# Some squares of batch 0's scores to Pool between its DMA issues, and the last weight blocks ahead of batch 1's second half

## The chip, the cores and the metric

The kernel runs on one core of one Trainium2 chip. The metric is the device time of one execution in microseconds. Before the change five runs took 436.14, 439.96, 436.26, 435.78 and 436.40 us, with a median of 436.26 us. Beside these there is one profiled execution, with its trace.

## The reference

Attention with squared ReLU in place of softmax, and behind it a gated feed-forward layer (FFN):

```
q, k, v: 8 batches x 12 heads x 448 x 64, float32
scores = (1/sqrt(64)) * q @ k^T
attn   = max(scores, 0)**2 / 448
x      = attn @ v                          # heads side by side: 3584 x 768
xn     = x / sqrt(mean(x*x) + 1e-6) * rms_g
h      = silu(xn @ w_gate) * (xn @ w_val)  # 3584 x 1536
out    = h @ w_out                         # 3584 x 768
```

There is no maximum and no sum over a row of scores, so a piece of scores can be rectified and squared alone, and used.

## The kernel before

**Tiling.** Heads go in pairs, six per batch. The two heads of a pair lie on the two halves of the 128 partitions, so that two 64-row matmuls run side by side in the array. Keys of a head are cut in three chunks of 128 and a rest of 64. Batch 0 is worked in two column halves of 224 queries (`NA`); batches 1 to 7 in one piece of 448.

**Stages of a batch.** q and k are transposed: for batches 0 and 1 by TensorE (`psT`), later ones by DMA. A unit of scores (`psS`, L869, two banks of PSUM wide) or the scores with the key rests of two pairs (`psR`, L890) is rectified into an SBUF tile `r` (L810 on VectorE or L812 on ScalarE), and `r` is squared in place (L818, VectorE alone: `SQ_ACT` is empty). A visit (`visit_aux`) takes two head pairs and multiplies their squares with v (`psAV`, L976); so a batch has three visits, and a half of batch 0 has three too. A visit has two halves with a hand-over between them; where the next visit's psR can be computed, it stands between the halves. What comes out is scaled into `xT`, its squares are summed (`psSS`), ScalarE makes `rstd`, and VectorE makes the six `xn` products (L1132). Then the FFN: `psg` and `psv` per block of 128 of the 1536 columns, `silu` on ScalarE (L1194), the product `hT` on VectorE (L1210), and the output projection `psO`.

**What sets the order.** The order of all engines is fixed while the program is built, by the class `Planner`. It holds estimated costs and due times and plays the engines forward: `choose` picks TensorE's next piece (visits first, then units of scores that are due, then the FFN stream), `engine_next` gives each elementwise task to an engine among those in its cost table. Until the first FFN matmul, TensorE is given filler matmuls (`psB`, L1481) where the planner sees a hole of more than `GAP` ns.[...]

**Loads.** All loads that cast from float32 to bfloat16 are issued by Pool, in the order of `FIRST`, then `ORDER`, then the two halves of `w_out`. In `ORDER`, `w0-2` is two 128-column blocks of both `w_gate` and `w_val` (786 KB read for each), `k` and `K` are the first and second half of batch 1's heads of k and q (three transfers each), and `v` is batch 1's v (two transfers). `issue` lets at most eight be in flight: each waits until the one eight places ahead of it has landed. Of batch 1, pairs 0 to 2 come with `k` and pairs 3 to 5 with `K`; all three visits need `v`.

**Banks.** PSUM starts with three wide buffers for scores and visits and two FFN banks. `warm` (L1492) turns the third wide buffer into two more FFN banks when the first half of batch 0 has had `THIRDV` visits.

Of the kernel before, what the change touches and what calls it, by code (L numbers as in the profile page):

```python
# [10 lines left out]
ALU = mybir.AluOpType  # L11
ACT = mybir.ActivationFunctionType
# [15 lines left out]
def latest(toks, at=0.0):  # L28
    for k in toks:
        if k.t is None:  # L30
            return None
        at = max(at, k.t)
    return at
# [21 lines left out]
class Planner:  # L55
# [2 lines left out]

    SEM, PSUM, HAND, SW = 50.0, 210.0, 200.0, 95.0
    WARM = 6500.0  # L60
    GAP = 160.0
    either = ("square", "squared")
    SLACK = 0.0
    PEN = 200.0
    acts = ("relu",)

# [23 lines left out]
    def engine_next(self):  # L90
        best = None
        for item in self.tasks:
            prio, seq, cost, emit, need, out, then = item
            r = latest(need)
            if r is None:
                continue
            for e in cost:
                s = max(r, self.free[e])
                if prio >= 2 and s + cost[e] > self.reserve[e] + 150.0:
                    continue  # L100
                if item[3].__name__ in self.either and e == "act" and s + cost[e] > max(r, self.free["dve"]) + cost["dve"] + self.SLACK:
                    continue
                key = (s + (self.PEN if e == "dve" and "act" in cost and item[3].__name__ in self.acts else 0.0), prio, seq)
                if best is None or key < best[0]:
                    best = (key, item, e, s)
        return best
# [155 lines left out]
    def choose(self, t):  # L262
# [21 lines left out]
        for a in self.auxes + self.sneaks:  # L284
            r = a.ready()
            if r is not None:
                times.append(r)
        if self.warm() and (not times or min(times) > t + self.GAP):
            return t, self.filler
# [51 lines left out]
def kernel(  # L341
# [11 lines left out]
    nc = tc.nc  # L353
# [18 lines left out]
    DUE1 = 1  # L372
    OLDSQ = 1
    SQ_ACT = range(0, 0)
    NA = 224
    HOLD = 900.0
    JOIN = 300.0
# [6 lines left out]
    W0 = (A2, A2, A3)  # L384
    WE = (A2, A2, A3)
    WO = (A2, A2, A2, A2)
    ORDER = "w0-2 w2-4 k w4-6 w6-8 w8-10 K w10-12 v"
    FIRST = "k4-8 q8-12 k8-12 v0-4 v4-12 Q"
    F32_T = 2
    AGATE = 6  # L390
    THIRD = 0
    THIRDV = 3
    CHAINS = range(0, 0)

    ctx.enter_context(tc.manual_schedule())
# [23 lines left out]
    def act_cost(n, per=0.8333):  # L419
        return 172.0 + per * n  # L420

    def dve_cost(n, per=1.0417):
        return 156.0 + per * n
# [98 lines left out]
    def load_k0(h0, h1):  # L522

        t = new_k0()

        def go():
            nc.gpsimd.dma_start(  # L527
                out=t[:, h0:h1], in_=src_of["k"][0, h0:h1].rearrange("h (p u) d -> p h (u d)", p=D)
            )

        landed("k", 0, h0, h1, issue(go, S * (h1 - h0) * D * 4, U * D * 4))
# [5 lines left out]
    def load_v(b, h0, h1, need=()):  # L537
        load_runs("v", b, h0, h1, low, 0, UH, need)
        load_runs("v", b, h0, h1, high, UH - 1, U, need)
# [76 lines left out]
    def free_bank(bank):  # L616
        def then(end):
            bank.free = end + 60.0
        return then
# [173 lines left out]
    live = {"r": 0}  # L793
    WR = max(S, max(n * min(512 // n, UH - 1) for n in (NA, S - NA)))
    xTs, x2s, accs, rstds, xns, hTs = {}, {}, {}, {}, {}, {}
    subs = [Sub(0, 0, NA, 0.0), Sub(0, NA, S - NA, 0.0)]
    subs += [Sub(b, 0, S, 0.0 if b < 2 else PACE) for b in range(1, B)]
# [3 lines left out]
    def rectify(sub, ps, bank, w, ready, put):  # L801

        got = {}
        tok = Tok()

        def relu(e):
            r = apool.tile([P, 2, WR], BF16, name="r", tag="r")
            got["r"] = r
            if e == "dve":
                nc.vector.tensor_relu(out=r[:, :, :w], in_=ps[:, :, :w])  # L810
            else:
                nc.scalar.activation(out=r[:, :, :w], in_=ps[:, :, :w], func=ACT.Relu)  # L812
            put(r, tok)

        def square(e):
            r = got["r"]
            if e == "dve":
                nc.vector.tensor_tensor(out=r[:, :, :w], in0=r[:, :, :w], in1=r[:, :, :w], op=ALU.mult)  # L818
            else:
                nc.scalar.activation(out=r[:, :, :w], in_=r[:, :, :w], func=ACT.Square)  # L820

        a = pl.task(
            PRIO_R, {"act": act_cost(2 * w), "dve": dve_cost(2 * w)}, relu, [Tok(ready)],
            None, free_bank(bank),
        )
        cost = {"dve": dve_cost(2 * w, 0.52)}
        if sub.b in SQ_ACT:
            cost["act"] = act_cost(2 * w, 0.9)
        pl.task(PRIO_R, cost, square, [a], tok)

    class Unit:
# [14 lines left out]
        def begin(self):  # L846
            sub, n = self.sub, self.sub.n
            bank = take_wide()
            ps = bank.take("psS")
            live["r"] += 1  # L850
            ends = []
            total = 2 * len(self.parts)
            w = n * len(self.parts)

            def put(r, tok):
                for j, c, o in self.parts:
                    sub.r[j, c] = (r, o, tok)

            def cb(t):
                ends.append(t)  # L860
                if len(ends) == total:
                    rectify(sub, ps, bank, w, max(ends), put)

            t = qkT[sub.b]
            for hh in range(2):
                prt = (low, high)[hh]
                for j, c, o in self.parts:
                    def emit(hh=hh, prt=prt, j=j, c=c, o=o):
                        nc.tensor.matmul(  # L869
                            out=ps[:, hh, o : o + n], lhsT=t[prt, j, 0, c * P : (c + 1) * P],  # L870
                            rhs=t[prt, j, 1, sub.q0 : sub.q0 + n], start=True, stop=True,
                        )
                    pl.ins[hh].append((n, emit, cb, 0.0))
# [7 lines left out]
    def rest_scores(sub, k, s):  # L881

        bank = take_wide()
        ps = bank.take("psR")
        live["r"] += 1
        n, t = sub.n, qkT[sub.b]
        for hh in range(2):
            prt = (low, high)[hh]
            for jj in range(2):
                nc.tensor.matmul(  # L890
                    out=ps[jj * D : (jj + 1) * D, hh, :n],
                    lhsT=t[prt, 2 * k + jj, 0, (UH - 1) * P : (UH - 1) * P + D],
                    rhs=t[prt, 2 * k + jj, 1, sub.q0 : sub.q0 + n],
                    start=True, stop=True,
                )

        def put(r, tok):
            sub.rest[k] = (r, tok)

        rectify(sub, ps, bank, n, s + n / 2.4 + pl.PSUM, put)  # L900
        sub.ready_rest[k] = True
# [462 lines left out]
    for x in FIRST.split():  # L1364
# [4 lines left out]
        else:  # L1369
            h0, h1 = [int(y) for y in x[1:].split("-")]  # L1370
            load_k0(h0, h1) if x[0] == "k" else load_v(0, h0, h1)
    for x in ORDER.split():
        if x[0] == "w":
# [118 lines left out]
    def warm():  # L1492
        if third in wide and getattr(subs[THIRD], "visited", 0) >= THIRDV and third.free is not None:
            wide.remove(third)
            early.close()
            psum_y = ctx.enter_context(
                tc.tile_pool(name="psum_y", bufs=1, space=bass.MemoryType.PSUM)
            )
            for x in range(2, 4):
                banks.append(Bank(psum_y, "m%d" % x, [P, 512]))  # L1500
                banks[-1].free = max(third.free, max(pl.t))
        return 0 not in started
# [33 lines left out]
```

## Time and profile before

| | |
|---|---|
| median of five runs | 436.26 us |
| profiled execution | 437.3 us, of it the profiled span 435.5 us |
| TensorE busy | 429.7 us (99%) |
| VectorE busy | 264.9 us (61%) |
| ScalarE busy | 251.8 us (58%) |
| Pool busy | 78.2 us (18%) |
| first FFN matmul | 24.66 us into the span |
| first visit of batch 1 | 52.46 us, held until 53.69 us |
| first FFN matmul of batch 1 | 84.18 us |

In the rows of the profile, an operation is named by line, engine, output <- inputs, then partitions x elements and type; "busy, mean ns of one" follow, and behind the last bar the idle time of the engine just before such operations and what ended it. In the chain and the timeline the first number is the start in us from the span's beginning and the second the length. TensorE's two half-array streams overlap, so matmuls in the timeline are longer than the slot by which they advance. A DMA row in the chain runs from issue to landing. In the rows with one digit per slice, the span is cut in 40 slices of 10.9 us, and a digit is the busy share in tenths.

### The profile page before, as it was taken

What the parts mean: (1) busy time and instruction counts of PE and PEld (TensorE: products, weight loads), DVE (VectorE), ACT (ScalarE), POOL (GpSimd) and SP (SyncE); (2) the same over time, 40 slices, a digit from 0 to 9 for tenths busy, and PEclk for the clock granted to TensorE, in tenths of its full rate; (3) what the DMA queues carried; (4) which work ended last, traced back from release to release, by engine and by line L of the source; (5) the groups of instructions that cost most, each with busy time, mean ns of one, the idle gap of its engine ahead of it and who ended that gap; (6) DMA issues with size and microseconds to landing.
All of it is one profiled execution on the core that took longest, in us unless ns stands there. A gap on an engine that the chain in (4) does not pass through costs nothing.

```text
span 435.5 us, 12544 instructions
## 1 busy us (share of the span) xinstructions
PE 429.7 (99%) x5573; PEld 314.8 (72%) x5573; DVE 264.9 (61%) x437; ACT 251.8 (58%) x356; POOL 78.2 (18%) x97
## 2 busy tenths in 40 slices
PE   8999999999999999999999999999999999999996
PEld 6688678964579755885579855795569955699996
DVE  3898873468754676657844578567754577442200
ACT  4878873576653675657743677476744567442222
POOL 7544311062160070005200340001000000000000
PEclk9999999999999999999999999999999999999999
DMA  9999999699799599188917992157103200020023
GB/s 146 192 197 197 203 193 115 133 166 124 114 152 203 118 137 66 38 133 105 129 38 158 143 158 16 32 124 94 28 14 100 74 2 2 2 74 2 2 74 108
DMA packets 134805, 44.68 MB, mean 103 GB/s; under 512 B 104096, under 2 KB 131296, under 8 KB 134752
## 3 DMA queue, kind: packets, MB, share of 16 engines
q0 software_dynamic: 94448, 24.16, 57.3%
q1 hardware_dynamic: 39808, 19.50, 21.7%
q8 instruction: 43, 0.70, 0.6%
q10 hardware_dynamic: 496, 0.24, 0.2%
q14 instruction: 10, 0.08, 0.1%
HBM read 48.76 MB, written 11.01 MB: 137 GB/s over the span
## 4 chain that ended last, share of the span: by engine, by line
PE 87%; DMA 11%; POOL 1%; issue 1%; ACT 0%; POOLq 0%
PE psO L147 26%; PE psv L147 24%; PE psg L147 23%; PE psAV L976 8%; PE psS L869 5%; DMA vb<-in_v_dram 3%; DMA wg_sb<-in_moe_w_gate_dram 3%; DMA wv_sb<-in_moe_w_val_dram 3%; DMA k<-in_k_dram 2%; PE psR L890 1%; PE psSS L1082 0%; POOL wg_sb L575 0%; POOL qb L496 0%; POOL k L527 0%; ACT ost L1288 0%
## 5 line engine op out<-in xcount | busy, mean ns | idle before, releaser
L147 PE MATMUL psv<-xn,wv_sb 64*128 64x448 bf16 (+1 forms) x1296 | 170.8, 329 | 0.0
L147 PE MATMUL psg<-xn,wg_sb 64*128 64x448 bf16 (+1 forms) x1296 | 170.2, 329 | 0.0
L812 ACT ACTIVATE r<-psS 128x896 bf16<-128x896 f32 x133 | 118.9, 919 | 32.8 <-PE psS L869 32.0
L147 PE MATMUL psO<-wo_sb,hT 64*128 64x384 bf16 (+2 forms) x1464 | 132.3, 310 | 0.0
L147 PEld LDWEIGHTS <-hT 64*128 64x128 bf16 x1464 | 109.9, 94 | 14.6 <-issue 2.5
L147 PEld LDWEIGHTS <-wv_sb 64*128 64x128 bf16 x1296 | 93.7, 94 | 31.8 <-issue 2.8
L147 PEld LDWEIGHTS <-wg_sb 64*128 64x128 bf16 x1296 | 94.8, 94 | 30.2 <-issue 2.9
L818 DVE TENSOR_TENSOR r<-r 128x896 bf16<-128x896 bf16 (+1 forms) x171 | 99.8, 610 | 11.1 <-ACT r L812 10.6
L1210 DVE TENSOR_TENSOR hT<-sil,psv 128x448 bf16<-128x448 bf16 x96 | 59.3, 618 | 62.5 <-PE psv L147 62.2
L1194 ACT ACTIVATE sil<-psg 128x448 bf16<-128x448 f32 x96 | 52.3, 545 | 47.8 <-PE psg L147 47.5
L869 PE MATMUL psS<-qkT 64*128 64x448 bf16 (+1 forms) x324 | 53.0, 329 | 0.0
L1288 ACT COPY ost<-psO 128x384 f32<-128x384 f32 (+2 forms) x51 | 23.0, 451 | 50.2 <-PE psO L147 50.0
L508 POOL DMA_DIRECT2D vb<-in_v_dram x18 | 13.1, 742 | 180.6 <-PE psg L147 75.3
L976 PE MATMUL psAV<-r,vb 64*64 64x448 bf16 (+1 forms) x756 | 43.5, 336 | 1.2 <-DMA vb<-in_v_dram 0.8
L1007 DVE TENSOR_SCALAR xT<-psAV 128x896 bf16<-128x896 f32 (+1 forms) x20 | 20.4, 1022 | 25.9 <-PE psAV L976 25.8
L812 ACT ACTIVATE r<-psR 128x896 bf16<-128x896 f32 (+1 forms) x23 | 19.6, 852 | 28.7 <-PE psR L890 28.7
L1132 DVE SCALAR_TENSOR_TENSOR xn<-xT,g_sb,rstd 128x448 bf16<-128x448 bf16 (+1 forms) x54 | 30.2, 628 | 7.8 <-ACT rstd L1116 7.7
L976 PEld LDWEIGHTS <-vb 64*64 64x64 bf16 x756 | 18.5, 106 | 21.6 <-PE psAV L976 8.5
L555 POOL DMA_DIRECT2D kb<-in_k_dram x42 | 31.5, 798 | 13.9 <-DMA vb<-in_v_dram 6.3
L869 PEld LDWEIGHTS <-qkT 64*128 64x128 bf16 x324 | 19.1, 94 | 9.7 <-issue 0.9
L810 DVE TENSOR_SCALAR r<-psS 128x896 bf16<-128x896 f32 x11 | 12.0, 1089 | 17.5 <-PE psS L869 17.4
L1032 DVE TENSOR_TENSOR x2f<-xT 128x896 f32<-128x896 bf16 x18 | 19.5, 1085 | 2.0 <-ACT xT L1005 2.0
(55 smaller groups left out, 176.3 us busy)
## 6 DMA issues: line engine op xcount, KB each, us to landing
vb<-in_v_dram POOLq DMA_DIRECT2D x14, 384.0 KB, 6.4
kb<-in_k_dram POOLq DMA_DIRECT2D x42, 96.0 KB, 7.3
qb<-in_q_dram POOLq DMA_DIRECT2D x6, 672.0 KB, 10.1
out_dram<-ost SPq DMA_DIRECT2D x7, 336.0 KB, 2.8
wg_sb<-in_moe_w_gate_dram POOLq DMA_DIRECT2D x6, 384.0 KB, 13.2
wv_sb<-in_moe_w_val_dram POOLq DMA_DIRECT2D x6, 384.0 KB, 13.2
wo_sb<-in_moe_w_out_dram POOLq DMA_DIRECT2D x2, 1152.0 KB, 19.3
out_dram<-ost SPq DMA_DIRECT2D x8, 288.0 KB, 2.9
```

The source lines that it names most:

```text
L147: mm = self.nc.tensor.matmul(out=seg.bank["tile"][:, off : off + seg.w], lhsT=lhsT[prt], rhs=rhs[prt], start=(seg.first and h == 0 and i = ...
L555: lambda o=o, i=i: nc.gpsimd.dma_start(out=o, in_=i),
L812: nc.scalar.activation(out=r[:, :, :w], in_=ps[:, :, :w], func=ACT.Relu)
L818: nc.vector.tensor_tensor(out=r[:, :, :w], in0=r[:, :, :w], in1=r[:, :, :w], op=ALU.mult)
L869: nc.tensor.matmul(out=ps[:, hh, o : o + n], lhsT=t[prt, j, 0, c * P : (c + 1) * P], rhs=t[prt, j, 1, sub.q0 : sub.q0 + n], start=True, st ...
L976: mm = nc.tensor.matmul(out=ps[hh * D : (hh + 1) * D, jj, :n], lhsT=vt[prt, 2 * (ja + jj) + hh, u * D : (u + 1) * D], rhs=r[prt, hh, o : o ...
L1007: nc.vector.tensor_scalar_mul(out=xT[at], in0=ps[:, :, :n], scalar1=inv_attn)
L1032: nc.vector.tensor_tensor(out=got["x2"][:], in0=xT[at], in1=xT[at], op=ALU.mult)
L1132: nc.vector.scalar_tensor_tensor(out=xn[:, kt, q0 : q0 + n], in0=xTs[b, 0][:, kt, q0 : q0 + n], scalar=g_sb[:, kt : kt + 1], in1=rstd[:, q ...
L1194: nc.scalar.activation(out=s[:, :m], in_=ps[:, :m], func=ACT.Silu)
L1210: nc.vector.tensor_tensor(out=h[:, fbs[0] : fbs[-1] + 1, o : o + n], in0=s[:, :m].rearrange("p (f s) -> p f s", s=n), in1=ps[:, :m].rearra ...
L1288: nc.scalar.copy(out=ost[:, c0 : c0 + w], in_=ps[:, :w])
```

## The change

A square of a batch in `SQ_POOL` (batch 0) may now be done by Pool too, at an estimated 105 + 1.755 ns an element in the planner's table. Pool takes one only where the planner sees it done no later than 400 ns (`POOL_SLACK`) after VectorE could have had it. In `ORDER`, `w10-12` changes places with `K`. Fillers are put in only for holes of more than 210 ns instead of 160, and the third wide buffer is given up after two visits instead of three.

```diff
-    GAP = 160.0
+    GAP = 210.0
     SLACK = 0.0
+    POOL_SLACK = 400.0
...
+                if e == "pool" and "dve" in cost and s + cost[e] > max(r, self.free["dve"]) + cost["dve"] + self.POOL_SLACK:
+                    continue
...
+    SQ_POOL = range(0, 1)
...
-    ORDER = "w0-2 w2-4 k w4-6 w6-8 w8-10 K w10-12 v"
+    ORDER = "w0-2 w2-4 k w4-6 w6-8 w8-10 w10-12 K v"
...
-    THIRDV = 3
+    THIRDV = 2
...
         def square(e):
             r = got["r"]
-            if e == "dve":
-                nc.vector.tensor_tensor(out=r[:, :, :w], in0=r[:, :, :w], in1=r[:, :, :w], op=ALU.mult)
+            if e == "act":
+                nc.scalar.activation(out=r[:, :, :w], in_=r[:, :, :w], func=ACT.Square)
             else:
-                nc.scalar.activation(out=r[:, :, :w], in_=r[:, :, :w], func=ACT.Square)
+                (nc.vector if e == "dve" else nc.gpsimd).tensor_tensor(
+                    out=r[:, :, :w], in0=r[:, :, :w], in1=r[:, :, :w], op=ALU.mult
+                )
...
+        if sub.b in SQ_POOL:
+            cost["pool"] = 105.0 + 1.755 * 2 * w
```

In the order that the planner now makes, Pool has four squares: the first (128x448) behind the second k transfer of `k`, the second (128x896) between the gate and the value weights of `w6-8`, the third (128x448) between those of `w10-12`, the fourth (128x448) between the two k transfers of `K`. Each is read by another visit of batch 0. TensorE has six filler matmuls fewer. From 41 us on, the transposes of batch 1's pairs 3 and 4 stand together and later, those of pair 5 stand behind batch 1's first visit, and FFN matmuls stand where they and some scores were. From batch 1's third visit on, TensorE's order is the old one. On VectorE and ScalarE the order changes with it, and some transposes' copies, rectifications and squares of `xT` change engine.

## The prediction

> **What bounds the kernel now.** The page comes first: what sets the end, and what else is full.
>
> ```profile
> PE 429.7 (99%) x5573; PEld 314.8 (72%) x5573; DVE 264.9 (61%) x437; ACT 251.8 (58%) x356; POOL 78.2 (18%) x97
> ...
> PE   8999999999999999999999999999999999999996
> ...
> DMA  9999999699799599188917992157103200020023
> ```
>
> TensorE has work in every slice; its idle time is 435.5 - 429.7 = 5.8 us, so a change that leaves TensorE's work alone can win only idle time, filler matmuls and changes between array shapes. But the DMA row is also full for the first six slices (10.9 us each). So I read the chain of work that ended last, in order of time, for the first 55 us:
>
> ```profile
> 4.11 6.66 DMA k<-in_k_dram
> ...
> 11.86 13.16 DMA wv_sb<-in_moe_w_val_dram
> ...
> 25.31 13.20 DMA wg_sb<-in_moe_w_gate_dram
> ...
> 38.79 14.85 DMA vb<-in_v_dram
> 53.64 0.04 issue
> 53.69 0.99 PE psAV L976 x14
> ```
>
> Until 53.64 us the chain is transfers, one behind the other: each is issued when the one eight places ahead of it has landed, and it lands 13 to 15 us later because the queue in front of it is that long. The last link is batch 1's v, whose second half lands at 38.79 + 14.85 = 53.64 us. From there on the chain is TensorE without a hole. The timeline of TensorE shows the meeting point:
>
> ```profile
> 52.46 0.38 PE L976 MATMUL psAV<-r,vb 64*64 64x448 bf16 x2
> 53.69 1.79 PE L976 MATMUL psAV<-r,vb 64*64 64x448 bf16 x26 [0.84 <-DMA vb<-in_v_dram]
> 55.28 0.39 PE L890 MATMUL psR<-qkT 64*64 64x448 bf16 x4
> 55.60 0.56 PE L147 MATMUL psv<-xn,wv_sb 64*128 64x224 bf16 x8
> ```
>
> Batch 1's first visit of the values (I call it AV1) comes up at 52.46 us, issues two matmuls and then stands until 53.69. **The end is therefore 53.69 us plus TensorE's work behind that point**, 435.53 - 53.69 = 381.8 us. What makes TensorE earlier at AV1 is worth nothing; what moves work from behind AV1 to ahead of it is worth its slots. Last, the windows by stage (columns: length, then busy time of PE, PEld, DVE, ACT, POOL):
>
> ```profile
> 0.00:24.66 24.66, 23.22 (x366) 15.85 (x367) 16.33 (x35) 16.94 (x24) 15.60 (x26) 1.00 1.30 172
> 24.66:40.00 15.34, 15.34 (x323) 12.49 (x324) 13.42 (x26) 10.95 (x16) 6.89 (x9) 1.00 1.46 197
> 40.00:53.64 13.64, 12.84 (x242) 10.35 (x238) 13.30 (x25) 12.54 (x18) 5.39 (x7) 1.00 1.40 200
> 53.64:86.61 32.97, 32.80 (x547) 27.72 (x549) 17.60 (x29) 17.86 (x25) 3.76 (x3) 1.00 1.27 148
> ```
>
> VectorE is 87% busy from 24.66 to 40 us and 98% until v lands, then 53%. A VectorE delay before 53.64 can reach TensorE; behind it there is room.
>
> **The change, part by part.** From the two built orders, engine by engine:
>
> (a) *Fillers.* Six of 75 filler matmuls go (9 to 5, 4 to 3, 17 to 16 in three runs between 15.67 and 24.66 us). Seventeen of them fill 22.88 to 24.66 us, 0.105 us each, so 0.63 us less TensorE time. All of it lies ahead of AV1, so alone it is worth 0: the wait for v grows by as much.
>
> (b) *Work on either side of AV1.* Behind AV1 the new order has 28 fewer 64x224 FFN matmuls, 4 more 64x448 score matmuls and 16 more transposes (head pair 5 of batch 1). Slots: two 224-wide matmuls advance by 0.096 us in the timeline, two 448-wide by 0.19; a block of 16 transposes takes from 44.42 to 44.97 us and, with the change of array shape in front, 0.62. So 28 x 0.048 = 1.34 us leave, 4 x 0.095 = 0.38 and 0.62 come: **-0.34 us behind AV1**. Ahead of it the same amounts come with the other sign, less about 0.19 because two pairs are now transposed in one block (one return to the other shape saved): +0.15 us.
>
> (c) *AV1 itself.* Now its two halves stand together and the four psR matmuls come after them; 53.69 to 55.60 is 1.91 us, its two first matmuls (0.09) having been done before. In the new order psR stands between the halves, as at 59.38 to 61.12 us: 1.74 us for all. Gain 1.91 - (1.74 - 0.09) = **0.26 us**, behind the landing.
>
> (d) *Last weights ahead of batch 1's second half of k and q.* Bytes ahead of v are the same, so v should land where it does, at 53.6 us. The weights for the last FFN blocks landed at 35.38 + 13.54 = 48.9 us and now land about 3.1 us earlier, which no one needs. The second half of k and q landed at 30.80 + 13.43 = 44.23 us; the pair of weights takes 48.92 - 44.23 = 4.7 us in the queue, so it lands at about 48.9 us. It is needed by the double block of transposes. TensorE reaches AV1 at 52.46 - 0.63 + 0.15 = 52.0 us if nothing holds it; between that block and AV1 stand 48 FFN matmuls (2.30 us), 4 score matmuls (0.38) and the block (1.0): it comes up at 48.3 us and waits about 0.6 to 0.7 us. TensorE then reaches AV1 at 52.7, still 0.9 us ahead of v. Cost 0 while that cover stands; without it 0.7 us. Queued behind the block on VectorE is one copy of it and, behind this, an hT product that frees an FFN bank: the same 0.7 us, same cover. Head pair 5 is transposed behind AV1, and its scores are needed by the third visit some 13 us later: 0.
>
> (e) *Four squares to Pool*, three of 128x448 and one of 128x896. The rows:
>
> ```profile
> L818 DVE TENSOR_TENSOR r<-r 128x896 bf16<-128x896 bf16 x165 | 97.6, 619 | 10.8 <-ACT r L812 10.3
> ...
> L818 DVE TENSOR_TENSOR r<-r 128x448 bf16<-128x448 bf16 x6 | 2.3, 386 | 0.4 <-ACT r L812 0.3
> ```
>
> VectorE loses 3 x 0.386 + 0.619 = 1.78 us of work. No such square runs on Pool. Below, Pool could be as fast as VectorE (0.39, 0.62). The nearest row is Pool's one elementwise operation on 128x128 in 0.29 us, 2.3 ns an element: 1.0 us for 448 and 2.0 us for 896, an estimate, which I take. Pool's queue holds them: the timeline of Pool (start, length, what, idle before) around the first two:
>
> ```profile
> 13.60 0.67 POOL L508 DMA_DIRECT2D kb<-in_k_dram  x1 [0.25 <-DMA vb<-in_v_dram]
> 15.36 0.77 POOL L496 DMA_DIRECT2D qb<-in_q_dram  x1 [1.09 <-DMA vb<-in_v_dram]
> ...
> 21.26 0.82 POOL L575 DMA_DIRECT2D wg_sb<-in_moe_w_gate_dram  x1 [1.13 <-DMA wv_sb<-in_moe_w_val_dram]
> 23.32 0.82 POOL L575 DMA_DIRECT2D wv_sb<-in_moe_w_val_dram  x1 [1.24 <-DMA wg_sb<-in_moe_w_gate_dram]
> ```
>
> The first square fits 14.27 to 15.36, the second runs 22.5 to 24.5 and makes the issue at 23.32 about 1.2 us late, the last two (rectified about 27.5 and 32 us) fall behind issues of 27 and 31 us. Those transfers land 13 us after issue because others are in front: an issue 1 to 2 us late only finds a shorter queue. Cost of the moved issues 0; that cover is 13 us thick. Their readers are four batch-0 visits; the first, now at 16.66 us and 0.4 us earlier without the four fillers, has its square at 15.3.
>
> [...] By VectorE's rows alone the step frees 1.78 us of VectorE. [...] 3 x 1.0 + 2.0 - 1.78 = +3.2 us of VectorE delay, the worst at 22.9 us, where six xn products gate the first FFN matmul at 24.66. TensorE has 53.6 - 52.0 = 1.6 us to lose before v lands[...]. I take 0: partial collisions, under the cover.
>
> (f) The earlier turn of one score bank into two FFN banks, and the new planner constants: nothing beyond the orders above. Sum: -0.34 - 0.26 = **-0.6 us**. The profiled span goes from 435.5 to 434.9, the profiled execution from 437.3 to 436.7; the median of the runs shown from 436.26 to 435.7.
>
> **Rivals.**
>
> *R1[...].* Pool's squares hold up VectorE, and through xn and the batch-0 squares TensorE. It decides from 1.6 us of TensorE lateness on. At the full 3.2 us: 435.7 + 1.6 = 437.3 us, slower than before; beyond 0.5% (2.2 us) only from 4.4 us, that is with Pool squares well over 2 us each. For it: VectorE 87 to 98% busy there.[...]
>
> *R2, k and q too late.* If their second half lands 2 us or more behind my 48.9, or the copies behind it stack up, AV1 comes after v: each us over the 0.9 of cover costs one. About 437.0. For it: landings here vary by 0.8 us for equal sizes (13.2 to 14.8). Against: the cover.
>
> *R3, v is not a wall.* If the new queue order lands v up to 1.6 us earlier, fillers and wait are won as well: 435.7 - 1.6 = 434.1. Against: same bytes, full queue.
>
> *R4, the change does nothing that counts*: VectorE's relief is hidden, the order shifts cancel, 436.3.
>
> **How the numbers follow.** The likeliest case 0.60 (435.7, give or take 0.7), R1 0.17, R2 0.09, R3 0.06, R4 0.08. About 0.5% (2.2 us) is what a measurement can tell from no change: faster is below 434.1, half of R3 and some of the likeliest case's edge, 0.06; slower is above 438.4, the ends of R1 and R2 (half of their 0.26), 0.13; same 0.81. The range holds the likeliest case, R4 and most of R1 and R2: 434.8 to 437.8.
>
> **What would show it.** Right: AV1 still waits for v at about 53.6 us; a short TensorE wait near 48.3 us for batch 1's q; behind AV1 about 381.2 us; Pool squares near 1 and 2 us. Wrong: v landing elsewhere, AV1 without a wait for v, VectorE squares and xn products stretched or idle beside Pool's squares by more than 1.6 us in all, or TensorE holes behind 54 us.

## The result and the profile after

The changed kernel takes 438.07 us, a median over 44 runs (the runs of the kernel before on the same chips: 436.29 us). The ratio is 1.0046, with a 95% interval of 1.0029 to 1.0063: about 1.8 us slower, where 0.6 us faster was forecast. Some executions of every version, the kernel before included, took 3 to 8 us longer at a mean granted clock of 0.98 to 0.99, and ratio and interval rest on most of these too, so a ratio here need not be that of the two medians. Its profiled execution took 437.63 us, its span 435.8 us.

The page of the changed kernel shows how busy each engine was, and TensorE's row of 10.9 us slices:

```profile
PE 429.1 (98%) x5567; PEld 314.5 (72%) x5567; DVE 268.1 (62%) x434; ACT 250.9 (58%) x355; POOL 83.3 (19%) x101
...
PE   8999999999999999999999999999999999999996
```

VectorE has three operations fewer than before (434 for 437), four squares of 1.78 us in all left it, and yet it is busy *longer*: 268.1 us for 264.9. By itself this says little, because other work changed engine too: VectorE has two more squares of `xT` in float32 (`x2f`, 20 for 18, 21.7 us for 19.5). The clearer sign is the chain of work that ended last, in order of time. Before, it ran through transfers until v landed at 53.64 us. Now:

```profile
14.16 1.04 DVE x L1026
15.20 1.01 DVE r L814
16.25 0.35 PE psB L1489 x2
...
23.07 3.61 DVE xn L1140 x6
26.72 0.83 PE psg L150 x7
```

Two stretches of VectorE have entered it, at 12 to 16 us and at 22.5 to 26.7 us, and no transfer stands in it behind these. The timeline of TensorE at batch 1's first visit (AV1 in the prediction):

```profile
54.49 0.95 PE L984 MATMUL psAV<-r,vb 64*64 64x448 bf16 x16
55.27 0.36 PE L898 MATMUL psR<-qkT 64*64 64x448 bf16 x4
55.50 0.79 PE L984 MATMUL psAV<-r,vb 64*64 64x448 bf16 x12
```

It begins at 54.49 us and shows no wait. v was issued at 38.54 and landed 13.3 us later, at 51.8 us, so 2.7 us ahead of its reader. The two halves of the visit stand around psR as forecast. From AV1's third matmul to the end of the span TensorE needs 381.35 us; before it was 381.85 us. So the work behind AV1 is 0.50 us shorter, close to the 0.60 us that the prediction counted, and all of the loss lies ahead of AV1. None of the waits that end TensorE's idle times in this trace ends with Pool: TensorE does not wait for the squares themselves.

Pool's timeline, with its four squares (in brackets the idle time before, and what ended it):

```profile
13.71 1.23 POOL L824 TENSOR_TENSOR r<-r 128x448 bf16<-128x448 bf16 x1 [0.19 <-DVE r L814]
...
22.63 1.98 POOL L824 TENSOR_TENSOR r<-r 128x896 bf16<-128x896 bf16 x1 [0.78 <-DVE r L814]
...
29.22 0.93 POOL L824 TENSOR_TENSOR r<-r 128x448 bf16<-128x448 bf16 x1 [1.32 <-ACT r L816]
...
33.64 0.93 POOL L824 TENSOR_TENSOR r<-r 128x448 bf16<-128x448 bf16 x1 [1.99 <-ACT r L816]
```

The estimates of 1.0 and 2.0 us were right. Beside these, VectorE's timeline:

```profile
13.54 0.61 DVE L824 TENSOR_TENSOR r<-r 128x896 bf16<-128x896 bf16 x1
14.07 1.12 DVE L1026 TENSOR_TENSOR x<-xT 128x448 bf16<-128x448 bf16 x1
...
22.99 3.68 DVE L1140 SCALAR_TENSOR_TENSOR xn<-xT,g_sb,rstd 128x224 bf16<-128x224 bf16 x6
26.59 1.68 DVE L824 TENSOR_TENSOR r<-r 128x896 bf16<-128x896 bf16 x3
...
29.67 0.72 DVE L1026 TENSOR_TENSOR x<-xT 128x448 bf16<-128x448 bf16 x1
```

In the kernel before, the same operations (lines L1018, L1132 and L818 there) read:

```profile
14.41 0.39 DVE L1018 TENSOR_TENSOR x<-xT 128x448 bf16<-128x448 bf16 x1
...
22.91 2.26 DVE L1132 SCALAR_TENSOR_TENSOR xn<-xT,g_sb,rstd 128x224 bf16<-128x224 bf16 x6
25.09 2.22 DVE L818 TENSOR_TENSOR r<-r 128x896 bf16<-128x896 bf16 x4
```

In this trace one operation of VectorE beside each of Pool's squares is held until about 0.25 us after that square: the square of `xT` at 14.07 us took 1.12 instead of 0.39 us, the six xn products 3.68 instead of 2.26 us (the first of them 1.87 instead of 0.44), the square of `xT` at 29.67 us 0.72, and one at 34.15 us 0.67 instead of 0.39. Together VectorE was held 0.73 + 1.42 + 0.34 + 0.28 = 2.77 us, against 1.78 us of work taken off it. What VectorE had begun 0.15 to 0.21 us ahead of a square of Pool's kept its length: two squares their 0.61 us, at 13.54 and 22.46 us, and two copies out of PSUM (`xT<-psAV`), at 29.01 and 33.49 us, their 0.63 and 0.62. It seems to go the other way too: Pool's first square began while VectorE's square of 13.54 us was running, and took 1.23 us where the later ones of its size took 0.93.

### The profile page after: what moved, and what is told of

Read it like the earlier page. It is cut to its first block, busy times and chain, and to the rows that moved or that the text cites. A ratio compares the mean times of both kernels' runs of the same rounds, so it can differ in the third digit from the quotient of the medians.

```text
span 435.8 us, 12535 instructions
## 1 busy us (share of the span) xinstructions
PE 429.1 (98%) x5567; PEld 314.5 (72%) x5567; DVE 268.1 (62%) x434; ACT 250.9 (58%) x355; POOL 83.3 (19%) x101
## 4 chain that ended last, share of the span: by engine, by line
PE 95%; DVE 2%; DMA 1%; issue 0%; ACT 0%; POOLq 0%
PE psO L150 26%; PE psv L150 26%; PE psg L150 25%; PE psAV L984 9%; PE psS L877 6%; PE psT L676 1%; DMA k<-in_k_dram 1%; PE psR L898 1%; DVE xn L1140 1%; DVE r L814 0%; DVE r L824 0%; DVE x L1026 0%; PE psSS L1090 0%; PE psT L674 0%; PE psB L1489 0%
## 5 line engine op out<-in xcount | busy, mean ns | idle before, releaser
L824 DVE TENSOR_TENSOR r<-r 128x896 bf16<-128x896 bf16 (+1 forms) x167 | 98.1, 614 | 11.1 <-ACT r L816 10.6
L816 ACT ACTIVATE r<-psR 128x896 bf16<-128x896 f32 (+1 forms) x24 | 20.5, 855 | 32.6 <-PE psR L898 31.7
L1015 DVE TENSOR_SCALAR xT<-psAV 128x896 bf16<-128x896 f32 (+1 forms) x21 | 21.5, 1025 | 28.2 <-PE psAV L984 28.2
L1140 DVE SCALAR_TENSOR_TENSOR xn<-xT,g_sb,rstd 128x448 bf16<-128x448 bf16 (+1 forms) x54 | 31.7, 654 | 7.8 <-ACT rstd L1124 7.7
L1040 DVE TENSOR_TENSOR x2f<-xT 128x896 f32<-128x896 bf16 x20 | 21.7, 1085 | 2.0 <-ACT xT L1013 2.0
## 6 DMA issues: line engine op xcount, KB each, us to landing
wv_sb<-in_moe_w_val_dram POOLq DMA_DIRECT2D x6, 384.0 KB, 13.5
```

The costliest lines, as they stand in the source:

```text
L824: (nc.vector if e == "dve" else nc.gpsimd).tensor_tensor(out=r[:, :, :w], in0=r[:, :, :w], in1=r[:, :, :w], op=ALU.mult)
L1015: nc.vector.tensor_scalar_mul(out=xT[at], in0=ps[:, :, :n], scalar1=inv_attn)
L1040: nc.vector.tensor_tensor(out=got["x2"][:], in0=xT[at], in1=xT[at], op=ALU.mult)
L1140: nc.vector.scalar_tensor_tensor(out=xn[:, kt, q0 : q0 + n], in0=xTs[b, 0][:, kt, q0 : q0 + n], scalar=g_sb[:, kt : kt + 1], in1=rstd[:, q ...
```

## The experiments

Each ran beside the kernel before, whose median in these comparisons is 436.19 to 436.28 us. The theory: Pool's squares hold VectorE, through it TensorE, and in an ordinary execution there is no wait for v to hide that. From the load order alone to the kernel with no square for Pool, each expectation gives this theory's figure first. Against it stand that the new orders of loads and matmuls delay TensorE (order theory), that visits wait for Pool's slower squares (late-result theory), that the squares hurt by making Pool's DMA issues late, and that v still sets the end and lands later. Some versions do work, beside that of the reference, that nobody reads.

**The kernel before, profiled a second time** (no edit).

> The kernel before, unchanged, for another profile of it. Question: is batch 1's v a wall in an ordinary execution? The profiled execution of before took 437.3 us, 1.0 us over the median of all its runs (436.3), and TensorE stood 1.2 us for v. Theory A (v is no wall as a rule): a profile near 436.2 us shows no wait for v, or one under 0.3 us. Theory B (v is a wall): the wait of about 1 us is there at any time. Ratio 1.000 for both.

436.22 us, ratio 0.9996 [0.9965, 1.0028], profiled execution 435.96 us with a span of 434.2 us. TensorE's timeline of it at AV1 (28 matmuls in one piece, and no wait in brackets):

```profile
51.60 0.78 PE L147 MATMUL psv<-xn,wv_sb 64*128 64x224 bf16 x12
52.30 1.81 PE L976 MATMUL psAV<-r,vb 64*64 64x448 bf16 x28
```

v was issued at 39.01 us and landed 13.3 us later, at 52.3 us, just as TensorE came up. The 1.2 us stand at AV1 in the profile shown with the prediction belonged to that one execution, whose 437.3 us were 1.0 us above the kernel's median. The work behind AV1 is 381.85 us in both.

**The load order alone.**

```diff
-    ORDER = "w0-2 w2-4 k w4-6 w6-8 w8-10 K w10-12 v"
+    ORDER = "w0-2 w2-4 k w4-6 w6-8 w8-10 w10-12 K v"
```

> The kernel before with the new load order alone (last weights ahead of batch 1's second half of k and q); no squares on Pool, old filler gap, old bank turn. [...] (the whole loss comes from Pool's squares holding up VectorE): 0 to -0.5 us, 435.8 to 436.3. Order theory (late k and q hold up the transposes and what follows): +1 us or more, 437.3 to 438.

436.20 us, 0.999 [0.9959, 1.0021], span 434.1 us. The second half of q landed at 48.0 us and TensorE did not stand for it. The load order is not the cause.

**All but the load order and the two planner constants.**

```diff
-    GAP = 210.0
+    GAP = 160.0
...
-    ORDER = "w0-2 w2-4 k w4-6 w6-8 w8-10 w10-12 K v"
+    ORDER = "w0-2 w2-4 k w4-6 w6-8 w8-10 K w10-12 v"
...
-    THIRDV = 2
+    THIRDV = 3
```

> The changed kernel with the old load order, the old filler gap and the old bank turn: squares on Pool alone. The planner puts the fourth square behind the first k transfer of the second half. [...] 437.5 to 438.3 us, with the xn products of batch 0's first half at 3.5 us for six in place of 2.3. Order theory: no change, 436.3.

437.84 us, 1.0048 [1.0021, 1.0075], span 436.4 us: 1.6 of the 1.8 us in the medians, and within its interval all of them, from the squares on Pool and the TensorE order that follows from them. The six xn took 3.7 us here too.

**The changed kernel, its squares put back on VectorE where they stand.** The planner still plans them for Pool, so TensorE's order is that of the changed kernel.

```diff
-                (nc.vector if e == "dve" else nc.gpsimd).tensor_tensor(
+                nc.vector.tensor_tensor(
```

> The changed kernel, TensorE's order and Pool's DMA order unchanged, but the four squares planned for Pool are issued on VectorE at the same places. [...] Pool holds nothing, VectorE gets 1.8 us of work back; 435.6 to 436.4 us. Order theory: as the changed kernel, 438.0. Late-result theory (readers wait for the slow Pool squares, VectorE isn't touched): 435.6 to 436.4 as well[...].

436.58 us, 1.0021 [0.9987, 1.0056], span 434.3 us. With the same TensorE order, 1.5 us of the 1.8 us are gone when Pool doesn't do the squares. How TensorE loses them can be followed up to the first FFN block. Executions begin unequally: the twelve `psS` near 13.5 us begin ahead of every square on Pool and of every filler that went, and already stand 0.35 us apart in the rows below, so times are counted from there. TensorE's timeline in the kernel before (second profile):

```profile
13.69 0.88 PE L869 MATMUL psS<-qkT 64*128 64x224 bf16 x12
...
24.49 0.27 PE L147 MATMUL psg<-xn,wg_sb 64*128 64x224 bf16 x1
...
24.81 1.21 PE L147 MATMUL psg<-xn,wg_sb 64*128 64x224 bf16 x11
25.86 0.35 PE L147 MATMUL psv<-xn,wv_sb 64*128 64x224 bf16 x2
```

In this one, with the new order and the squares on VectorE:

```profile
13.34 0.88 PE L877 MATMUL psS<-qkT 64*128 64x224 bf16 x12
...
23.96 0.27 PE L150 MATMUL psg<-xn,wg_sb 64*128 64x224 bf16 x1
...
24.43 1.61 PE L150 MATMUL psg<-xn,wg_sb 64*128 64x224 bf16 x11
25.88 0.35 PE L150 MATMUL psv<-xn,wv_sb 64*128 64x224 bf16 x2
```

And in the changed kernel, where the bracket gives the idle time before the first and what ended it:

```profile
13.53 0.88 PE L877 MATMUL psS<-qkT 64*128 64x224 bf16 x12
...
25.00 0.25 PE L150 MATMUL psg<-xn,wg_sb 64*128 64x224 bf16 x1 [0.35 <-DVE xn L1140]
...
25.29 2.26 PE L150 MATMUL psg<-xn,wg_sb 64*128 64x224 bf16 x11
27.39 0.35 PE L150 MATMUL psv<-xn,wv_sb 64*128 64x224 bf16 x2
```

The block's gate matmuls need the xn products one after the other. In the kernel before the first one starts 10.80 us behind the twelve psS and the psv matmuls 12.17 us behind them. With the squares on VectorE the first one starts after 10.62 us, 0.18 us earlier, by the fillers that went. But psv comes after 12.54 us, 0.37 us later, for the large square, at the place where it was planned for Pool, now stands between the first xn product and the other five. VectorE's timeline of that kernel:

```profile
22.37 0.45 DVE L1140 SCALAR_TENSOR_TENSOR xn<-xT,g_sb,rstd 128x224 bf16<-128x224 bf16 x1
22.73 0.62 DVE L824 TENSOR_TENSOR r<-r 128x896 bf16<-128x896 bf16 x1
23.26 1.90 DVE L1140 SCALAR_TENSOR_TENSOR xn<-xT,g_sb,rstd 128x224 bf16<-128x224 bf16 x5
```

With the squares on Pool the first gate matmul starts after 11.47 us, the eleven behind it take 2.26 us, and psv comes after 13.86 us: 1.32 us later than with the squares on VectorE, 1.69 us later than in the kernel before. In the medians the two kernels with the same TensorE order are 1.49 us apart (438.07 against 436.58 us).

**Only the three squares of 128x448 on Pool.**

```diff
-        if sub.b in SQ_POOL:
+        if sub.b in SQ_POOL and w == NA:
```

> The changed kernel, but only the three 128x448 squares may go to Pool; the 128x896 square stays on VectorE. TensorE's order as in the changed kernel. [...] the 896 square is the one that meets the xn products (about 1.6 us of TensorE holes at 25 to 26.7 us of some 2.6), so 436.2 to 436.9 us. If the other squares cost as much: 437.5 or more.

436.67 us, 1.002 [0.9991, 1.005], span 435.0 us. In the medians it is not to be told from the one with all squares on VectorE (+0.1 us). Its six xn took 2.25 us. In its profile the small squares do hold VectorE, though: beside the first one, five squares took 3.67 us instead of 2.52:

```profile
15.21 3.67 DVE L824 TENSOR_TENSOR r<-r 128x896 bf16<-128x896 bf16 x5
```

Its psv came 12.99 us behind the twelve psS, 0.45 us later than with all squares on VectorE.

**Only the square of 128x896 on Pool**, the others issued on VectorE.

```diff
-                (nc.vector if e == "dve" else nc.gpsimd).tensor_tensor(
...
+                (nc.gpsimd if e == "pool" and w != NA else nc.vector).tensor_tensor(
```

> TensorE's order and the plan of the changed kernel; only the 128x896 square runs on Pool, the three of 128x448 are issued on VectorE at the same places. [...] the changed kernel (438.1) less the three small squares, which cost about 0.1 to 0.3 us (all on VectorE: 436.6; small ones alone on Pool: 436.7): 437.6 to 438.1, with the xn products at 3.6 us for six. If the large square isn't the one: 436.6 to 437.0.

437.69 us, 1.0024 [0.9993, 1.0054], span 435.8 us. Pool's timeline of it, and then VectorE's:

```profile
22.52 1.82 POOL L827 TENSOR_TENSOR r<-r 128x896 bf16<-128x896 bf16 x1
```

The six products beside it:

```profile
22.72 3.68 DVE L1143 SCALAR_TENSOR_TENSOR xn<-xT,g_sb,rstd 128x224 bf16<-128x224 bf16 x6
```

The one square stretches the six xn by as much as all four did. Its psv came 13.42 us behind the twelve psS: 0.9 of the 1.32 us by which the squares on Pool delay it come from this square, and the other 0.4 us, at the first visit behind it, from the first small one. By the medians it carries 1.1 of the 1.5 us; the intervals overlap, so the rows carry this reading more than the medians do.

**The kernel before, with four products added on Pool that nobody needs.** They stand at the places of the four squares, read and write a tile of their own, and wait for nothing but Pool's queue.

```diff
+    scr = const.tile([P, 2 * S], BF16, name="scr", tag="scr")
+    nc.vector.memset(scr[:], 1.0)
+    def beside(n):
+        nc.gpsimd.tensor_tensor(out=scr[:, :n], in0=scr[:, :n], in1=scr[:, :n], op=ALU.mult)
...
+            if nm == "k" and b == 1 and (h0 == 0) == (u0 == UH):
+                beside(S)
...
+                if dst is wg_sb and f0 in (6, 10):
+                    beside(2 * S if f0 == 6 else S)
```

> The kernel before with four Pool products on a scratch tile that nobody reads (448, 896, 448 and 448 elements), put between the DMA issues near where the changed kernel has its squares; VectorE keeps all its squares. [...] VectorE's two-input operations are stretched beside them; 437.0 to 439 us, xn products held. Late-result theory: nobody waits for them, 436.3. Issue theory (late DMA issues cost): as in scratch_memset.

442.27 us over only six runs, 1.0129 [1.0078, 1.018], with a profiled execution of 445.66 us in which TensorE's granted clock was 0.50 from 10 to 20 us (last section). That mixes two effects, so it was run again, longer:

> The four scratch products beside the kernel before again, for more executions and a profile with TensorE's clock granted from the start. [...] 440.1 us, 3.9 over before. Pool's four products last 4.55 us in all; the hold is at most that. The changed kernel has the hold and, against it, 1.8 us less on VectorE: 3.9 - 1.8 = 2.1, near its +1.8.

440.58 us, 1.0092 [1.0066, 1.0119], span 438.2 us, clock 0.998. VectorE kept all its own squares here, so this is the hold without the relief. Pool's timeline:

```profile
14.08 0.95 POOL L437 TENSOR_TENSOR scr<-scr 128x448 bf16<-128x448 bf16 x1
...
21.95 1.69 POOL L437 TENSOR_TENSOR scr<-scr 128x896 bf16<-128x896 bf16 x1
```

VectorE's timeline beside it:

```profile
14.00 1.30 DVE L1028 TENSOR_TENSOR x<-xT 128x448 bf16<-128x448 bf16 x1
...
21.43 2.48 DVE L828 TENSOR_TENSOR r<-r 128x448 bf16<-128x448 bf16 x1 [0.32 <-ACT r L822]
...
25.36 3.38 DVE L1142 SCALAR_TENSOR_TENSOR xn<-xT,g_sb,rstd 128x224 bf16<-128x224 bf16 x6
```

A square of 0.39 us took 2.48 us beside a Pool product of 1.69 us, and ended 0.27 us after it. No data passes between the two engines' operations here: the hold needs no dependency. It costs 4.4 us in the medians.

**The same places, but memsets in place of products**: Pool only writes, for as long (1.02, 1.76, 1.03 and 1.02 us in pairs).

```diff
-        nc.gpsimd.tensor_tensor(out=scr[:, :n], in0=scr[:, :n], in1=scr[:, :n], op=ALU.mult)
+        for _ in range(2):
+            nc.gpsimd.memset(scr[:, :n], 1.0)
```

> As the scratch products, but at each of the four places Pool does two memsets of the same tile, which read nothing. [...] 436.3 us, no stretched operation on VectorE. If any Pool work beside VectorE costs, or if the later DMA issues do: 437 or more.

436.36 us, 1.0008 [0.9982, 1.0034], span 434.0 us. Pool's timeline at the second place:

```profile
21.85 1.76 POOL L438 MEMSET scr<- 128x896 bf16 x2
```

VectorE's timeline a moment later:

```profile
22.57 2.25 DVE L1143 SCALAR_TENSOR_TENSOR xn<-xT,g_sb,rstd 128x224 bf16<-128x224 bf16 x6
```

Pool is as occupied, its DMA issues stand behind work of the same length, and nothing is lost that shows. So late issues don't explain the loss, and Pool's writes don't either. What is left is that Pool *reads* SBUF.

**The same places, with two copies each**: Pool reads one input.

```diff
+        nc.gpsimd.tensor_copy(out=scr[:, :n], in_=scr[:, :n])
+        nc.gpsimd.tensor_copy(out=scr[:, :n], in_=scr[:, :n])
```

> The kernel before with two Pool copies of the scratch tile at each of the four places where the scratch products stood: Pool reads one input in place of two. If any Pool read holds VectorE's two-input operations for its length: 437.5 us or more (products 440.2, memsets 436.4), in proportion to Pool's copy time. If it takes two inputs on Pool's side: 436.4.

437.73 us, 1.0033 [1.0004, 1.0062], span 436.6 us. Two of the copies in Pool's timeline:

```profile
22.54 0.94 POOL L437 COPY scr<-scr 128x896 bf16<-128x896 bf16 x1
23.54 0.99 POOL L438 COPY scr<-scr 128x896 bf16<-128x896 bf16 x1
```

And in VectorE's, a square whose record begins 0.57 us ahead of the first copy's and ends 0.25 us after it, 1.76 us for 0.39:

```profile
21.97 1.76 DVE L829 TENSOR_TENSOR r<-r 128x448 bf16<-128x448 bf16 x1 [0.32 <-ACT r L823]
```

One input is enough. Two copies out of PSUM that begin beside Pool's copies, at 29.85 and 34.34 us, kept their 0.62 us. This time the six xn fell behind the copies (2.25 us), and the cost is less than the products'.

**The changed kernel with no square for Pool in the planner.** The load order and the two planner constants remain.

```diff
-    SQ_POOL = range(0, 1)
+    SQ_POOL = range(0, 0)
```

> All of the change but the squares on Pool: new load order, filler gap 210, bank turn after two visits, planned anew. [...] 435.6 to 436.3 us, equal to or a little better than before. Order theory: 437.5 to 438.

436.07 us, 1.0003 [0.9981, 1.0025], span 434.0 us. No slower than the kernel before, and not to be told from it; no version here is measurably faster than that one.

**v and the last weight blocks exchange places in the queue** (kernel before, all other orders kept).

```diff
+    ring = []
+    def turned(fn):
+        k = len(ring)
+        ring.append(fn)
+        return lambda: ring[(k + 2) % 4]()
...
-        landed(nm, b, h0, h1, issue(go, D * (h1 - h0) * run, run, need))
+        landed(nm, b, h0, h1, issue(turned(go) if nm == "v" and b == 1 else go, D * (h1 - h0) * run, run, need))
...
-            tok = issue(go, P * KT * (f1 - f0) * P * 4, (f1 - f0) * P * 4)
+            tok = issue(turned(go) if f0 == 10 else go, P * KT * (f1 - f0) * P * 4, (f1 - f0) * P * 4)
```

> The kernel before with every engine's order kept, but batch 1's v and the last weight blocks change places in Pool's queue, so that v lands some 4.7 us earlier, near 48 us. If v were a wall in ordinary executions, TensorE would reach its first visit of batch 1 without it and win up to 1.2 us: 435.0 to 435.6. If v lands just as TensorE comes (52.3 and 52.3 us in the second profile of before), 436.0 to 436.3, and the slowest of the undisturbed runs a little faster.

440.15 us, 1.0072 [1.0049, 1.0095]. As a test of whether v bounds the end it is lost, for another wait took over. TensorE's timeline:

```profile
47.70 0.35 PE L876 MATMUL psS<-qkT 64*128 64x448 bf16 x2
...
50.89 0.36 PE L147 MATMUL psg<-xn,wg_sb 64*128 64x224 bf16 x1 [2.83 <-DMA wg_sb<-in_moe_w_gate_dram]
```

TensorE comes to the last weight blocks just after 48 us, and then stands 2.83 us for their gate half. In the kernel before that half was issued at 33.06 us (second profile), landed 13.2 us later, at 46.3 us, and so stood ready.

**What v's landing really hides.** Fifteen fillers of 0.105 us (1.6 us), directly ahead of AV1:

```diff
+            if (b, k) == (1, 0):
+                for _ in range(15):
+                    nc.tensor.matmul(
+                        out=ps[:, 0, :HALF], lhsT=nc.const_aps.tensor(1.0, [P, P], BF16),
+                        rhs=nc.const_aps.tensor(1.0, [P, HALF], BF16), start=True, stop=True,
+                    )
```

> The kernel before with 15 filler matmuls (0.105 us each, 1.6 us) directly ahead of batch 1's first visit: TensorE comes later by 1.6 us, all else as it was. If v's landing covers a late TensorE as the prediction had it (up to 1.2 us of wait in the first profile), +0.4 us: 436.6. If v lands as TensorE comes (52.2 against 51.9 to 52.9 in the other profiles), most of it is paid: +1.2 to +1.6 us, 437.4 to 437.9.

437.62 us, 1.0034 [1.0022, 1.0047]: +1.38 us. And the same fifteen ahead of batch 1's second visit, where no transfer can hide them:

```diff
-            if (b, k) == (1, 0):
+            if (b, k) == (1, 1):
```

> The same 15 fillers directly ahead of batch 1's second visit, where no transfer can cover them: +1.6 us, 437.8, whatever the cover ahead of the first visit. The difference between the two runs is the cover.

437.86 us, 1.0042 [1.0029, 1.0055]: +1.62 us, the fillers' own length. Ahead of AV1 all but 0.24 us of it counted, a difference that lies within the two intervals. Had v covered 1.2 us in an ordinary execution, as in the first profile, the run ahead would have lost some 0.4 us, and its interval begins at 1.0. So the cover is small and may be none. That v still set the end falls with this, and by the landing itself: over the fifteen profiles in which v is last in the queue it landed between 51.8 and 53.6 us, and in the changed kernel at 51.8, the earliest of all.

## Why the prediction was wrong

**"The end is therefore 53.69 us plus TensorE's work behind that point": this step failed, and the rest hung on it.** The second half, 381.8 us behind AV1, was right and held in the second profile (381.85). The first half was read from one execution, in which v came 1.2 us behind TensorE. The prediction gave both numbers, 437.3 us for this execution and 436.26 for the median, and asked nothing of the 1.0 us between them. That excess was about the wait: in the second profile, with an execution of 435.96 us, v and TensorE met to within 0.1 us, and the added fillers left a cover of 0.24 us or none. The 1.6 us that TensorE was to have in hand ahead of v were not there.

**(e), the squares on Pool, "I take 0: partial collisions, under the cover": both halves failed.** The 3.2 us weighed there were the author's estimate for the case that each of Pool's squares holds VectorE for its own length: 3 x 1.0 + 2.0 = 5.0 us, less 1.78. No trace of the kernel before showed a hold. The trace of the changed kernel does: holds of 0.73, 1.42, 0.34 and 0.28 us, and beside memsets none (six xn in 2.25 us). That is 2.77 us and not 5.0, though Pool's four squares lasted 5.07: the beginning of each fell beside an operation of VectorE that kept its length. Less the relief of 1.78 us this is 1.0 us of VectorE time net, and yet TensorE came to the first psv 1.69 us later than before. The sum of hold minus relief was the wrong measure. Up to the last of the xn products, for which TensorE waits, VectorE was held 0.73 + 1.42 = 2.15 us and was relieved of the first small square alone; the large square had stood behind them (four squares at 25.09 us before, three at 26.59 us now), where its going won TensorE nothing that shows. The prediction named that place ("the worst at 22.9 us, where six xn products gate the first FFN matmul") and did not price it by itself; priced there, at the estimated 2.0 us of the large square and with no cover, it would have turned the forecast of 435.7 into 437.7 us.

**(a) Fillers: too large, and its fate wrong.** 0.63 us was forecast for the first FFN matmul. It starts 0.53 us earlier with the squares on VectorE, but 0.35 us of that stand there already at the twelve psS, ahead of all fillers that went; 0.18 us is their gain (0.15 us in the kernel with no square for Pool, 24.45 - 13.80 = 10.65 for 10.80 us). It was to be lost in the wait for v. It is lost at once: in that kernel psv stands 12.17 us behind the twelve psS, as before.

**(b) and (c), the work on either side of AV1: right.** -0.34 and -0.26 us behind AV1 were forecast, -0.50 measured (381.85 to 381.35), in three profiles with this order alike. The +0.15 us ahead of AV1 came out larger. From the psv matmuls to AV1 the changed kernel takes 54.49 - 27.39 = 27.10 us, the same order with the squares on VectorE 27.09, the kernel before 52.30 - 25.86 = 26.44 us: +0.66 us. About 0.48 us of it is a hole ahead of a psR in a batch-0 visit (36.69 to 37.58 us; before 35.16 to 35.57), the rest is close to the forecast. The profile names no engine or transfer that ends the hole, and its cause stays open. So the new order, with the squares on VectorE and the large one among its xn products, has a span of 434.3 us against 434.2 before, in spite of the 0.50 us behind AV1.

**(d), the load order: cost 0 right, details wrong.** q landed at 47.8 us in the changed kernel, not 48.9, and there was no wait: the double block of transposes came up at 50.6 us there, and at 49.1 with the squares on VectorE, not at 48.3. That no one needs the last weights earlier agrees with the load order alone (436.20 us).

**Pool's durations and issues: right.** 0.93 to 1.23 and 1.98 us against 1.0 and 2.0; that late issues cost nothing agrees with the memsets.

**The sum with measured terms.** All from the rows of one profile each, in us:

| kernel | twelve psS begin | first psv | between |
|---|---|---|---|
| before (second profile) | 13.69 | 25.86 | 12.17 |
| no square for Pool | 13.80 | 25.97 | 12.17 |
| squares back on VectorE | 13.34 | 25.88 | 12.54 |
| three small squares on Pool | 13.36 | 26.35 | 12.99 |
| large square on Pool | 13.70 | 27.12 | 13.42 |
| changed | 13.53 | 27.39 | 13.86 |

From the kernel before to the changed one, 1.69 us are lost by the first psv, some 1.3 through the large square and 0.4 through the first small one; 0.66 by the order from there to AV1; 0.50 come back behind it. That makes 1.85 us; the medians say 1.8. The two spans are 1.6 us apart, for the profiled execution of the changed kernel reached the twelve psS 0.16 us earlier.

**The rivals.** R1 is what happened, at 438.07 for its 437.3 us: Pool's squares held up VectorE, by 2.77 us, and through it TensorE. Why they hold it was not shown. Its price, 1.6 us, is near the loss of 1.8 us partly by luck: it was 3.2 us of delay less a cover of 1.6, and the runs show 1.69 us of delay and next to no cover. Its limit ("it decides from 1.6 us of TensorE lateness on") hung on the cover that didn't exist, and so did its chance of 0.17. R2 did not occur; the landings it cites, 13.2 to 14.8 us, vary by 1.6 us and not by 0.8. R3 asked whether v is a wall: it is scarcely one, but without the squares on Pool the kernel stays at 436.1 us, and what bounds it there was not separated (TensorE and v meet at 52.3 us in that profile too). R4 is what the change would be without Pool.

## What to carry to other kernels

Before a wait is used as cover, see whether it stands in an execution at the median, and if the forecast rests on it, put known filler work ahead of it and behind it: the difference is the cover. Work moved from VectorE to Pool need not be off VectorE: here 1.78 us of squares went, and Pool's squares held VectorE's squares and xn products for 2.77 us. Price such a move by what VectorE has to do in that very stretch, and look for stretches in which it is idle or copies out of PSUM (0.62 us a copy beside Pool's copies, as elsewhere). A relief spread over an engine doesn't pay for a hold at the one place that another engine waits for. Two profiles are compared from a point that the change can't have touched, not from the start of the span.

## What the runs showed of the hardware

**VectorE's squares and xn products were held beside Pool's products and copies, and not beside its memsets.** Pool's four products (4.53 us in all) cost the kernel 4.4 us, copies, with one read input, 1.5 us, and memsets of about the same length (4.83 us) 0.1 us, which is within their interval. The order in which the records begin doesn't settle which of the two engines is held: in the changed kernel VectorE's squares of 0.61 us that began 0.17 us ahead of Pool's kept their length, but in two other runs a VectorE square of 0.39 us whose record begins 0.5 to 0.6 us ahead of Pool's (21.43 and 21.95 us, 21.97 and 22.54 us) took 2.48 and 1.76 us, until 0.25 to 0.27 us after Pool's end. Why was not tried.

**TensorE's granted clock was at one half behind a stand of 1.94 us.** In the profiled execution of the first run with scratch products, TensorE stood 1.94 us for the first k transfer, directly after its first matmuls. Its timeline:

```profile
6.96 0.41 PE L680 MATMUL psT<-ident,k 64*64 64x64 bf16 x14 [1.94 <-DMA k<-in_k_dram]
```

The window behind it (length, busy time of PE, PEld, DVE, ACT, POOL, granted clock, DMA share, GB/s), with TensorE never idle and its clock at 0.50:

```profile
10.00:15.00 5.00, 5.00 (x78) 2.84 (x76) 3.91 (x6) 3.45 (x4) 5.00 (x8) 0.50 1.58 191
```

The mean granted clock was 1.00 up to 5 us, 0.72 from 5 to 10, 0.50 from 10 to 20, 0.91 from 20 to 25 and 1.00 from 25 to 45: one half from 7.2 to 20.9 us, by an estimate from these means. This execution took 445.66 us where three others of the same kernel took 440.1 to 441.1 and two 443.4 and 444.2. With v early, the mean clock was 1.00 from 45 to 50 us, 0.57 from 50 to 54, over the end of the stand of 2.83 us at 50.89 us, and 1.00 from 54 to 58; that version lost 4.0 us, more than the stand. In the changed kernel TensorE stood 0.73 us for the first k transfer, and the mean clock was 1.00 from 0 to 30 us. What makes the clock fall was not tried.
